# A Fourier mix and a squared-ReLU layer on one core: the order and size of the folding pieces on VectorE and ScalarE

## The chip, the core and the metric

The kernel runs on one core of a Trainium2 chip. The core has five engines with a queue of instructions each: TensorE (PE in the profile, with PEld for its weight loads), VectorE (DVE), ScalarE (ACT), GpSimd (POOL) and SyncE (SP), which here issues the loads and stores. An engine works through its own queue in order and waits on semaphores for the others. TensorE writes its results to PSUM; VectorE and ScalarE read them there, GpSimd does not.

The metric is the device time of one execution in microseconds (us), the lower the better. Every time in this document is in us unless ns is written.

## What is computed

```python
def _attn_ref(x):                       # x: 8 x 3008 x 256, float32
    X = np.fft.fft(x, axis=1)
    X = np.fft.fft(X, axis=2)
    return X.real.astype(np.float32)

def _moe_ref(x, w_in, w_out):           # x: 24064 x 256; w_in 256 x 2048; w_out 2048 x 256
    h = x @ w_in
    r = np.maximum(h, 0.0)
    g = r * r
    return (g @ w_out).astype(np.float32)
```

The first result, as 24064 rows of 256, is the second function's x. The tables of cosines and sines are made on the host from the sizes alone.

## The kernel before

**Folding.** The 3008 rows of a batch are used four at a time: rows n, S-n, M-n and M+n (M is S/2) have the same cosines and sines up to sign, so their sums and differences are formed first. 753 such groups of four make seven tiles of up to 128 partitions (`class_tiles`; the first four are the classes of even and of odd-even n, the last three, from `ODD0`, the odd class). `fold(b, t)` returns the pieces of work for batch b and tile t, each with a cost in units that a planner uses:

- `f_s` and `f_d` (L345, L349): sums and differences of the rows, two at a time, 512 elements.
- `f_sc` and `f_dc` (L355, L356, L360): the same along the 256 columns, column d with column D-d; the columns 0 and 128, which have no partner, are copied (L355).
- `f_p` and `f_q` (L370, L375): the folded tile `w`, in two parts of the columns (`PART`: 129 and 127) and two parities kp.
- for tiles 5 and 6 of a later batch, which share a class that is split once more, `f_turn` (a shuffle on VectorE, a copy on ScalarE, L395), `f_even` (two VectorE operations, L407 and L408, then `sine`: four ScalarE multiplications, L403) and `f_odd` (two VectorE operations, L415, which read what `sine` wrote).

`f_d` also issues the load of the tile three places later.

**Transform.** `dft_ops(b)` lists the row transform in groups: matmuls (L440, L485) into `pd`, ScalarE copies (L448, L489) and VectorE sums and differences (L453 to L457, L497 to L501) into `Pt` and `Qt`, 1505 columns, and `Et` for the column 128, which is gathered from all later batches at once: `load_column` loads it (28 small DMAs), `fold_column` folds it tile by tile (L327, L330), `dft_ops(None)` transforms it.

**Layer.** The column transform is multiplied into w_in once (`G1`, `G2`, `gE`). Then each batch has six blocks of 251 columns of `Pt` and `Qt` (the last has 250) and each block eight steps j. The loop at the end goes through all 8 x 6 x 8 = 384 steps i. In a step, `front` does two halves: two matmuls into `ph` (L536, L537), then on VectorE `he` (L539) and the two parts of `g` (L541, L542), then a call of `between()`. After that come the stores that are due, then `back` for the step two before (`LAG` = 2): seven matmuls (L589) into the accumulators mA to mD, which exist once. Last comes `combine`: Relu and Square on ScalarE (L551, L552) and four GpSimd operations that make `s` (L559 to L562). After the eighth step of a block, `gather` copies mA and mB to SBUF on ScalarE (L605, L607) and combines them with mC and mD on VectorE (L610 to L612) and GpSimd (L614 to L622). Because of the lag this happens in the step with j = 1 of the next block; TensorE may begin mA of the new block, one step later, when L605 has read the old one. The two stores of a block follow in steps 3 and 4, with VectorE transposes (L649, L650) and DMAs on SP.

**The planner.** While batch b is in the loop, the pieces that prepare batch b+1 (`ahead`) are in the list `side`. `between()` takes `pace` from `spent` and, while `spent` is not above zero, takes pieces from the list and adds their cost. `pace` is the sum of the costs over the number of calls, less six. In the first batch it begins at step 8, at half pace for the first eight steps. Steps 0 to 7 still bring in the weights (`load_win`, `load_wout`), whose `convert` splits a float64 into float32 on VectorE and ScalarE (L227 to L240).

**The start.** Batch 0 has nothing to hide its preparation behind. The pieces are called in an order written out by hand: `for_p(t)` calls the pieces 0, 2 and 4 of tile t (s, sc, p), `for_q(t)` the pieces 1, 3 and 5, with groups of the transform between. Buffers: `fs`, `fd`, `sc`, `dc` two each (`fp`), `s` three (`sp`), PSUM's `h` and `d` two each.

Of the kernel before, what the change touches and what calls it, by code (L numbers as in the profile page):

```python
# [13 lines left out]
P = 128  # L14
# [67 lines left out]
def kernel(  # L82
# [120 lines left out]

    raws = 0

    def convert(dst, src):
# [4 lines left out]
        if src.dtype == F32:  # L211
            w = fp.tile([P, 2, CH], F32, name="fs", tag="fs")
# [10 lines left out]
        m = fp.tile([P, 2, CH], F32, name="fs", tag="fs")  # L223
# [22 lines left out]
    def load_win(j):  # L246
# [4 lines left out]
        def products():  # L251
# [11 lines left out]
            nc.scalar.copy(gE[:, j::NJ], ps[:, 0:2])  # L263
# [49 lines left out]
    xe, we = {}, {}  # L313
    e_dram = dp.tile([NE, NKT], F32, name="e_dram")

    def load_column(t):

        _, r0, step, rows = TILES[t]
        xe[t] = const.tile([P, 4, NE], F32, name=f"xe{t}")
        for i in range(4):  # L320
            nc.sync.dma_start(out=xe[t][0:rows, i], in_=x[1:B, r0:r0 + step * (rows - 1) + 1:step, i, H].rearrange("b r -> r b"))

    def fold_column(t):
        r = slice(0, TILES[t][3])
        v = xe[t]
        s = hp.tile([P, 2, NE], F32, name="es", tag="es", bufs=2)
        tt(out=s[r], in0=v[r, 0::2], in1=v[r, 1::2], op=ALU.add)  # L327
        we[t] = const.tile([P, 2, NE], F32, name=f"we{t}")
        for kp in range(2):
            tt(out=we[t][r, kp], in0=s[r, 0], in1=s[r, 1], op=ALU.subtract if kp else ALU.add)  # L330

    def fold(b, t):
# [10 lines left out]
        def f_s():  # L343
            v = xt[b, t]
            tt(out=new(fp, "fs", [P, 2, D])[r], in0=v[r, 0::2], in1=v[r, 1::2], op=ALU.add)  # L345

        def f_d():
            v = xt[b, t]
            tt(out=new(fp, "fd", [P, 2, D])[r], in0=v[r, 0::2], in1=v[r, 1::2], op=ALU.subtract)  # L349
            if b > 0 and b * NT + t + NX < B * NT:  # L350
                load_x(*divmod(b * NT + t + NX, NT))

        def f_sc():
            s, sc = st["fs"], new(fp, "sc", [P, 2, H + 1])
            nc.vector.tensor_copy(sc[r, :, 0:H + 1:H], s[r, :, 0:H + 1:H])  # L355
            tt(out=sc[r, :, 1:H], in0=s[r, :, 1:H], in1=s[r, :, D - 1:H:-1], op=ALU.add)  # L356

        def f_dc():
            d = st["fd"]
            tt(out=new(fp, "dc", [P, 2, H - 1])[r], in0=d[r, :, 1:H], in1=d[r, :, D - 1:H:-1], op=ALU.subtract)  # L360
# [6 lines left out]
        def f_p():  # L367
            sc, w = st["sc"], w_of(t)
            for kp in range(2):
                tt(out=w[r, kp, PART[0]], in0=sc[r, 0], in1=sc[r, 1], op=ALU.subtract if kp else ALU.add)  # L370

        def f_q():
            dc, w = st["dc"], w_of(t)
# [473 lines left out]
```

## Time and profile before

| what | us |
|---|---|
| median of 6 runs | 1968.94 |
| the runs | 1967.08 to 1969.64 |
| the profiled execution | 1967.04 |
| its span, first to last instruction | 1965.3 |

Busy time by stage, from the table of stretches (TensorE's granted clock is a share of full speed):

| stretch | PE | DVE | ACT | POOL | clock |
|---|---|---|---|---|---|
| 0 to 110: load, batch 0, first block | 83.06 | 92.40 | 53.08 | 0.71 | 0.94 |
| 110 to 245 (135 us): batch 1 prepared | 134.15 | 124.85 | 66.31 | 84.74 | 1.00 |
| 245 to 1655 (1410 us) | 1406.52 | 1067.01 | 668.90 | 899.23 | 1.00 |
| 1655 to the end (311 us) | 301.95 | 175.63 | 139.03 | 183.27 | 0.99 |

How to read it: a busy share says where an engine had an instruction under way. A matmul's record lasts longer than the distance to the next one (0.375 against 0.21), so short pauses of TensorE hide in the overlap, and the distance from start to start is the better measure. A line of the timeline gives the start, the time taken, engine, source line, operation, what is written from what, the count, and in brackets the idle time before it with what ended that. A line of the list of waits gives engine, tensor and line, what it waited for, the total, how often, and the longest.

### The profile page before, as it was taken

To read this page: it belongs to the slowest core of one execution; us is meant where nothing else is said; L and a number is where in the kernel's file an instruction comes from. 1 tells how busy PE (TensorE), PEld (TensorE's weight loads), DVE (VectorE), ACT (ScalarE), POOL (GpSimd) and SP (SyncE) were. 2 spreads that over 40 slices of the span, in tenths; PEclk is the share of its full clock that TensorE was granted. 3 is DMA by queue.
4 is the path that set the end of the run, shared out by engine and by line. 5 is a ranking of instruction groups with operands and counts; after the bars stand their busy time and mean duration, and the time that the engine had idled before them with its cause. 6 is when DMAs were issued, how large, how long until landed. Compare 5 with 4: busy or idle time off the path is not lost.

```text
span 1965.3 us, 27667 instructions
## 1 busy us (share of the span) xinstructions
PE 1925.7 (98%) x9160; PEld 1705.1 (87%) x9160; DVE 1459.9 (74%) x3606; ACT 927.3 (47%) x1075; POOL 1168.0 (59%) x1702
## 2 busy tenths in 40 slices
PE   5999999999999999999999999999999999999998
PEld 3788888888988889888898888888898888988887
DVE  7889967887678876887768886787867887655554
ACT  1754544454445544545444454444544454444443
POOL 0037645667466765676557665666756676556564
PEclk8999999999999999999999999999999999999999
DMA  7332101110011110111011100121001100000000
GB/s 197 108 45 52 27 13 44 45 27 25 29 34 33 32 25 27 41 35 33 11 35 37 45 19 11 37 52 27 20 16 51 33 11 22 27 11 11 22 11 22
DMA packets 145341, 68.89 MB, mean 35 GB/s; under 512 B 129003, under 2 KB 136110, under 8 KB 145197
## 3 DMA queue, kind: packets, MB, share of 16 engines
q1 hardware_dynamic: 144121, 66.60, 13.1%
q8 instruction: 72, 1.18, 0.3%
q14 instruction: 72, 0.59, 0.1%
q10 hardware_dynamic: 1076, 0.52, 0.1%
HBM read 42.39 MB, written 24.68 MB: 34 GB/s over the span
## 4 chain that ended last, share of the span: by engine, by line
PE 91%; DVE 5%; ACT 2%; DMA 1%; issue 1%; POOL 0%; SPq 0%; DVEq 0%; ACTq 0%; POOLq 0%
PE mA L589 16%; PE mC L589 16%; PE ph L537 16%; PE ph L536 16%; PE mB L589 16%; PE mD L589 8%; PE pd L440 2%; PE pd L485 2%; DVE he L539 1%; DVE g L542 1%; DVE g L541 1%; DMA cosT<-in_cos_s_dram 1%; ACT g L551 0%; ACT g L552 0%; DMA xt<-in_x_dram 0%
## 5 line engine op out<-in xcount | busy, mean ns | idle before, releaser
L551 ACT ACTIVATE g<-g 128x1004 f32<-128x1004 f32 (+1 forms) x384 | 399.3, 1040 | 797.9 <-DVE g L542 456.7
L559 POOL TENSOR_TENSOR s<-g 128x251 f32<-128x251 f32 (+1 forms) x376 | 241.2, 641 | 713.2 <-ACT g L552 675.9
L539 DVE SCALAR_TENSOR_TENSOR he<-Et,gE,ph 128x251 f32<-128x251 f32 (+1 forms) x768 | 361.2, 470 | 388.2 <-PE ph L537 387.3
L536 PE MATMUL ph<-Pt,G 128*128 128x251 f32 (+1 forms) x1536 | 451.4, 375 | 4.3 <-ACT G L256 3.4
L537 PE MATMUL ph<-Qt,G 127*128 127x251 f32 (+1 forms) x1536 | 451.3, 374 | 0.4 <-DVE Qt L453 0.4
L552 ACT ACTIVATE g<-g 128x1004 f32<-128x1004 f32 (+1 forms) x384 | 399.3, 1040 | 12.2
L589 PE MATMUL mA<-g,wout 128*128 128x251 f32 (+1 forms) x1504 | 380.4, 374 | 3.5 <-ACT sA L605 3.5
L589 PE MATMUL mC<-s,wsum 128*128 128x251 f32 (+1 forms) x1504 | 381.7, 375 | 0.0
L541 DVE TENSOR_TENSOR g<-he,ph 128x251 f32<-128x251 f32 (+1 forms) x768 | 320.4, 417 | 54.9 <-DVE he L539 1.0
L536 PEld LDWEIGHTS ph<-Pt,G 128*128 128x128 f32 x1536 | 288.2, 189 | 41.7 <-ACT G L256 4.0
L537 PEld LDWEIGHTS ph<-Qt,G 127*128 127x128 f32 x1536 | 291.1, 190 | 36.6 <-DVE Qt L453 0.8
L589 PEld LDWEIGHTS mA<-g,wout 128*128 128x128 f32 x1504 | 281.9, 189 | 40.0 <-ACT sA L605 5.8
L589 PEld LDWEIGHTS mC<-s,wsum 128*128 128x128 f32 x1504 | 285.7, 190 | 34.6
L542 DVE TENSOR_TENSOR g<-he,ph 128x251 f32<-128x251 f32 (+1 forms) x768 | 314.2, 409 | 0.0
L560 POOL TENSOR_TENSOR s<-s,g 128x251 f32<-128x251 f32 (+1 forms) x376 | 289.8, 771 | 29.5
L561 POOL TENSOR_TENSOR s<-g 128x251 f32<-128x251 f32 (+1 forms) x376 | 293.1, 780 | 0.0
L562 POOL TENSOR_TENSOR s<-g,s 128x251 f32<-128x251 f32 (+1 forms) x376 | 253.5, 674 | 0.0
L589 PE MATMUL mB<-g,wsum 128*128 128x251 f32 (+1 forms) x752 | 220.5, 374 | 0.0
L589 PE MATMUL mD<-s,wout 128*128 128x251 f32 (+1 forms) x752 | 220.3, 374 | 0.0
L589 PE MATMUL mB<-s,wout 128*128 128x251 f32 (+1 forms) x752 | 219.9, 374 | 0.0
L589 PEld LDWEIGHTS mB<-g,wsum 128*128 128x128 f32 x752 | 142.6, 190 | 17.4
L589 PEld LDWEIGHTS mD<-s,wout 128*128 128x128 f32 x752 | 141.9, 189 | 17.7
(117 smaller groups left out, 1354.4 us busy)
## 6 DMA issues: line engine op xcount, KB each, us to landing
out_dram<-os SPq DMA_DIRECT2D x376, 56.0 KB
xt<-in_x_dram SPq DMA_DIRECT2D x32, 384.0 KB
xt<-in_x_dram SPq DMA_DIRECT2D x42, 128.0 KB
Et<-e_dram SPq DMA_DIRECT2D x7, 752.5 KB
xt<-in_x_dram SPq DMA_DIRECT2D x9, 512.0 KB
out_dram<-os SPq DMA_DIRECT2D x288, 6.8 KB
raw<-in_moe_w_in_dram SPq DMA_DIRECT2D x16, 256.0 KB
raw<-in_moe_w_out_dram SPq DMA_DIRECT2D x16, 256.0 KB
```

What stands on the lines that cost most here:

```text
L536: nc.tensor.matmul(hP, G1[:, fs], pt[:, ks], start=True, stop=True)
L537: nc.tensor.matmul(hQ, G2[:, fs], qt[:, ks], start=True, stop=True)
L539: nc.vector.scalar_tensor_tensor(out=t, in0=et[:, ks], scalar=gE[:, fc:fc + 1], in1=hP, op0=ALU.mult, op1=ALU.add)
L541: tt(out=g[:, h, 0, 0:n], in0=t, in1=hQ, op=ALU.add)
L542: tt(out=g[:, h, 1, 0:n][:, ::-1], in0=t, in1=hQ, op=ALU.subtract)
L551: act(v, v, AF.Relu)
L552: act(v, v, AF.Square)
L559: gt(out=s1, in0=g21, in1=g22, op=ALU.add)
L560: gt(out=s2, in0=s1, in1=g11, op=ALU.subtract)
L561: gt(out=s3, in0=g11, in1=g21, op=ALU.subtract)
L562: gt(out=s4, in0=g12, in1=s2, op=ALU.subtract)
L589: nc.tensor.matmul(acc[nm][:, i, 0:n], w, v[:, 0:n], start=j == 0 and i == 0, stop=j == NJ - 1, skip_group_check=True)
```

## The change

- `fold`: column D of the sums is a column of zeros in two constant buffers (`sums`), so that one operation forms all 129 sums of `f_sc`; column 0 gets x + 0, column 128 gets twice its value. The differences are taken in another order (`0::3` less `1:3`), so that both parts of the columns have the same sign in the last step; for batches after the first, `f_sc` and `f_dc` write one tile and `f_w` forms all 256 columns of a parity in one operation. The costs are new.
- The factor two of column 128 is balanced: `gE` is halved where it is made, and the separately loaded columns are doubled (`nc.scalar.mul(xe, xe, 2.0)`). They lie in one tile `xe`, set to zero on GpSimd, and are folded in three VectorE operations for all seven tiles.
- `convert` takes its scratch from the pool of `s` rather than from `fs`.
- `sine` becomes a piece of its own, after `f_even` and before `f_odd`.
- `between()` does nothing in the steps with j = 1, and `pace` is worked out for the calls that are left.

```diff
+    sums = [const.tile([P, 2, D + 1], F32, name=f"fs{i}") for i in range(2)]
+    for v in sums:
+        nc.gpsimd.memset(v[:, :, D:], 0.0)
...
+    def scratch():
+        return sp.tile([P, 4 * CK], F32, name="m", tag="s")[:, 0:2 * CH].rearrange("p (c e) -> p c e", c=2)
...
-        m = fp.tile([P, 2, CH], F32, name="fs", tag="fs")
+        m = scratch()
...
-            nc.scalar.copy(gE[:, j::NJ], ps[:, 0:2])
+            nc.scalar.mul(gE[:, j::NJ], ps[:, 0:2], 0.5)
...
-    xe, we = {}, {}
+    xe = const.tile([P, 4, NT, NE], F32, name="xe")
+    we = const.tile([P, 2, NT, NE], F32, name="we")
+    nc.gpsimd.memset(xe, 0.0)
...
-    def fold_column(t):
-        r = slice(0, TILES[t][3])
-        v = xe[t]
-        s = hp.tile([P, 2, NE], F32, name="es", tag="es", bufs=2)
-        tt(out=s[r], in0=v[r, 0::2], in1=v[r, 1::2], op=ALU.add)
-        we[t] = const.tile([P, 2, NE], F32, name=f"we{t}")
+    def fold_columns():
+        nc.scalar.mul(xe, xe, 2.0)
+        s = hp.tile([P, 2, NT, NE], F32, name="es", tag="es", bufs=1)
+        tt(out=s, in0=xe[:, 0::2], in1=xe[:, 1::2], op=ALU.add)
         for kp in range(2):
-            tt(out=we[t][r, kp], in0=s[r, 0], in1=s[r, 1], op=ALU.subtract if kp else ALU.add)
+            tt(out=we[:, kp], in0=s[:, 0], in1=s[:, 1], op=ALU.subtract if kp else ALU.add)
...
         def f_s():
+            nonlocal folds
+            st["fs"] = sums[folds % 2]
+            folds += 1
             v = xt[b, t]
-            tt(out=new(fp, "fs", [P, 2, D])[r], in0=v[r, 0::2], in1=v[r, 1::2], op=ALU.add)
+            tt(out=st["fs"][r, :, 0:D], in0=v[r, 0::2], in1=v[r, 1::2], op=ALU.add)
 
         def f_d():
             v = xt[b, t]
-            tt(out=new(fp, "fd", [P, 2, D])[r], in0=v[r, 0::2], in1=v[r, 1::2], op=ALU.subtract)
+            tt(out=new(fp, "fd", [P, 2, D])[r], in0=v[r, 0::3], in1=v[r, 1:3], op=ALU.subtract)
...
+        def halves():
+            if b == 0 or "sc" not in st:
+                st["sc"] = fp.tile([P, 2, D], F32, name="sc", tag="sc")
+            return st["sc"]
+
         def f_sc():
-            s, sc = st["fs"], new(fp, "sc", [P, 2, H + 1])
-            nc.vector.tensor_copy(sc[r, :, 0:H + 1:H], s[r, :, 0:H + 1:H])
-            tt(out=sc[r, :, 1:H], in0=s[r, :, 1:H], in1=s[r, :, D - 1:H:-1], op=ALU.add)
+            s = st["fs"]
+            tt(out=halves()[r, :, PART[0]], in0=s[r, :, 0:H + 1], in1=s[r, :, D:H - 1:-1], op=ALU.add)
 
         def f_dc():
             d = st["fd"]
-            tt(out=new(fp, "dc", [P, 2, H - 1])[r], in0=d[r, :, 1:H], in1=d[r, :, D - 1:H:-1], op=ALU.subtract)
+            tt(out=halves()[r, :, PART[1]], in0=d[r, :, 1:H], in1=d[r, :, D - 1:H:-1], op=ALU.subtract)
...
-        def f_p():
-            sc, w = st["sc"], w_of(t)
+        def f_w(part=slice(0, D)):
+            v, w = st["sc"], w_of(t)
             for kp in range(2):
-                tt(out=w[r, kp, PART[0]], in0=sc[r, 0], in1=sc[r, 1], op=ALU.subtract if kp else ALU.add)
-
-        def f_q():
-            dc, w = st["dc"], w_of(t)
-            for kp in range(2):
-                tt(out=w[r, kp, PART[1]], in0=dc[r, 0], in1=dc[r, 1], op=ALU.add if kp else ALU.subtract)
-
-        ops = [(0.9, f_s), (0.9, f_d), (1.2, f_sc), (0.6, f_dc), (0.9, f_p), (0.7, f_q)]
+                tt(out=w[r, kp, part], in0=v[r, 0, part], in1=v[r, 1, part], op=ALU.subtract if kp else ALU.add)
+
+        if b == 0:
+            return [f_s, f_d, f_sc, f_dc, lambda: f_w(PART[0]), lambda: f_w(PART[1])]
+        ops = [(0.9, f_s), (0.9, f_d), (0.7, f_sc), (0.6, f_dc), (1.1, f_w)]
...
             tt(out=v, in0=a, in1=w, op=ALU.add)
             tt(out=w, in0=a, in1=w, op=ALU.subtract)
+
+        def f_sine():
             sine(spare("f1", "f1"), st["w"], (0, 1))
             sine(spare("f2", "f0"), st["v"], (1, 0))
...
-        return ops + [(0.8, f_turn), (1.2, f_even), (1.4, f_odd)]
+        return ops + [(0.8, f_turn), (1.3, f_even), (0.2, f_sine), (1.4, f_odd)]
...
-        return (folds + [start] + [(0.6, lambda t=t: fold_column(t)) for t in range(NT)] + dft_ops(None) + tables
+        return (folds + [start] + [(1.5, fold_columns)] + dft_ops(None) + tables
...
-        if i < NJ:
+        if i < NJ or i % NJ == LAG - 1:
             return
...
-                spent, pace = 0.0, sum(t for t, _ in side) / (2 * per - 6 - (0 if i else 3 * NJ))
+                calls = 2 * (NJ - 1) * len(BLOCKS) - 6
+                spent, pace = 0.0, sum(t for t, _ in side) / (calls - (0 if i else 3 * (NJ - 1)))
```

## The prediction

> **What bounds the kernel now.** I read the page first (engine shares, the 40 slices), then TensorE's own waits after 110 us, then the timelines of PE, ACT and DVE around each wait, last the start. The page:
>
> ```profile
> span 1965.3 us, 27667 instructions
> ...
> PE 1925.7 (98%) x9160; PEld 1705.1 (87%) x9160; DVE 1459.9 (74%) x3606; ACT 927.3 (47%) x1075; POOL 1168.0 (59%) x1702
> ...
> PE   5999999999999999999999999999999999999998
> ...
> PE 91%; DVE 5%; ACT 2%; DMA 1%; issue 1%; POOL 0%; SPq 0%; DVEq 0%; ACTq 0%; POOLq 0%
> ```
>
> TensorE is the bound from the second slice to the last but one; VectorE, whose folds the diff rewrites, has a quarter of the span free. So VectorE time saved is worth nothing by itself; only TensorE's stalls and the start can give. TensorE's waits from 110 us to the end:
>
> ```profile
> PE mA L589 <- ACT sA L605: 3.5, 6, 0.8
> PE ph L536 <- DVE g L542: 0.8, 2, 0.7
> PE po L638 <- DVE c L616: 0.5, 1, 0.5
> ```
>
> Nine waits in 1855 us; the third is the tail, which the diff leaves alone. The six of the first line lie about 235 us apart (478, 712, 947, 1181, 1416, 1651), one per batch that is prepared. One of them, PE then ACT:
>
> ```profile
> 712.17 0.59 PE L537 MATMUL ph<-Qt,G 127*128 127x251 f32 x2
> 713.29 1.11 PE L589 MATMUL mA<-g,wout 128*128 128x251 f32 x4 [0.54 <-ACT sA L605]
> 714.25 0.38 PE L589 MATMUL mB<-g,wsum 128*128 128x251 f32 x1
> ...
> 712.09 0.69 ACT L403 ACTIVATE f<-w,turn 60x129 f32<-60x129 f32 x2 [1.97 <-DVE w L408]
> 712.69 0.56 ACT L605 COPY sA<-mA 128x502 f32<-128x502 f32 x1
> ```
>
> TensorE may not start the new block's mA before ScalarE has copied the old one (L605). ScalarE had stood still for 1.97 us in front of the second pair of multiplications of `sine`, since these wait for VectorE's L408, and L605 is queued behind them. A pair of matmuls normally starts every 0.425 us (four 0.85). Here mA starts 713.29-712.17=1.12 after the pair before, 0.69 late, and mB 0.96 after mA, 0.11 late: the stall costs 0.80 us, more than the idle 0.54. Five are like this; the sixth (1650.50 to 1651.90, then 0.96) costs 0.97+0.11=1.08. Sum 5.08.
>
> The second line of waits, PE:
>
> ```profile
> 239.76 0.59 PE L537 MATMUL ph<-Qt,G 127*128 127x251 f32 x2
> 241.05 0.69 PE L536 MATMUL ph<-Pt,G 128*128 128x251 f32 x2 [0.70 <-DVE g L542]
> ...
> 211.30 0.59 PE L537 MATMUL ph<-Qt,G 127*128 127x251 f32 x2
> 212.04 0.69 PE L536 MATMUL ph<-Pt,G 128*128 128x251 f32 x2 [0.15 <-DVE g L542]
> ```
>
> Counted alike, 1.29-0.43+0.10=0.96 and 0.74-0.43+0.10=0.41. In both VectorE was behind: from 236.96 to 239.75 it does the tiny `fold_column` operations, and at 212 the `even` pair and two transposes.
>
> **The change, part by part.** *(a) ScalarE's sine later, gather steps free.* The step counter can be replayed from the code. Before: 54.2 units over 90 calls is 0.602 a call; ahead of the last `f_even` stand 40.6 units, so it is popped at call 68, step 33 of 48, and 33 mod 8 = 1 is the step with the gather: exactly the six stalls. After: 47.8 units over 78 calls, 0.613 a call, 14 calls per block; ahead of the last `f_sine` stand 35.2, call 58, the second call of step 32, one step before the gather; `f_even` goes at step 31. So L408 is long done, and in step 32 ScalarE has 1.4 us of sine (two rows of 0.69) and 2.1 us of Relu and Square in 4.67 us, nothing else ahead of L605. **-5.08.**
>
> What is late next? The other tile: `f_sine` (27.3 units ahead, call 45) and `f_odd` (27.5, call 45) are popped in one call, the first of step 26, just after a gather step. VectorE's L415 waits there for ScalarE, with half 1's he and g queued behind it, and TensorE's next ph for those. From the clean gather step that starts at 631.41: sA starts 2.75 later, sB ends 4.2 later; Relu and Square (1.04 each) then end at 6.3, the two sine pairs at 7.0 and 7.65. VectorE has half 0's g at 7.05 and ends two L415 (0.72 mean) by 8.5, half 1's three (1.2) by 9.7; TensorE needs them at 10.2. Margin 0.5, so 0; range 0 to 0.4 for each of seven batches.
>
> *(b) Fewer fold operations in the main loop.* Per tile, L355 goes (0.27 mean), four L370/L375 (0.53 and 0.58) become two of 256 elements. No such row exists; L407 and L408, same shape, take 0.47 and 0.81 in the mean. So a tile costs 5.26 now and 3.72 to 4.41 after. Hidden behind TensorE; it matters only while batch 1 is prepared, where VectorE is 93% busy (110 to 210 us). A block of eight steps has 37.4 us; 16 halves of 1.16, the gather's three (1.2) and four transposes (1.7) leave 15.9. Before, 16 calls of 0.976 units at 1.01 us: 15.8, hence the 0.41 stall. After, 14 calls of 0.970 at 0.89 to 1.05: 12.1 to 14.3. Both L536 stalls should go, **-0.41** and, since `fold_columns` is 3 DVE operations (nearest row 128x94 0.25) for 21, **-0.96**. Its ScalarE multiplication (128x196; between 0.19 of 128x1 and 0.50 of 128x377) comes a step after the gather, before VectorE gets there; its DMAs were issued 90 us earlier, in the same places on SP's queue. But steps 26 to 28 are the heaviest: each 2.3 for the halves, then sc, dc and w (1.9 to 2.9); turn, even and two transposes (2.5 to 3.2); odd and two transposes (2.3). Added up with a step of 4.67, the carry into step 29 is 0.1 to 1.4, and there half 1's g, with the next f_s (0.85) in front, comes 1.2 before TensorE needs it or 0.2 after. I take **+0.2** (0 to 0.8, about half of the two stalls).
>
> *(c) The start.* Up to 20 us everything waits for the cosT DMA, so the first five L355 gave nothing. Two more are on the path (DVE, DVE, PE):
>
> ```profile
> 25.29 0.17 DVE L355 COPY sc<-fs 128x4 f32<-128x4 f32 x1
> ...
> 28.06 0.17 DVE L355 COPY sc<-fs 120x4 f32<-120x4 f32 x1
> ...
> 29.08 5.13 PE L440 MATMUL pd<-cosT,w 120*128 120x377 f32 x14 [1.15 <-DVE w L370]
> ```
>
> Each takes 0.21 from its start to the next one's, so L440 starts 0.42 earlier and VectorE, which is never idle for 0.3 from 33.5 to 52.3, carries that on. The granted clock was 0.50 from 20 to 30 us and 0.77 from 30 to 35, that is, it rose at about 32.3. If the rise follows the matmuls, 0.42 is gained; if it stays, the six cold matmuls after 29.1 (0.63 each, warm 0.32) gain about half. I take **-0.25**, midway, range 0 to -0.5. [...] From 53 to 106 us the loop of 8.5 us a step (Relu, Square, G, fd, then win, he, g) keeps all its members; gE as a multiplication rather than a copy is 0.19 (128x1 row) against 0.175, **+0.1** over six. The conversions' scratch tile only moves to the pool of s, which GpSimd first uses at step 8, when the conversions are over. Three memsets on an idle GpSimd before 9 us: 0.
>
> **Sum**: -5.08-0.41-0.96+0.2-0.25+0.1 = -6.4 against this execution's 1967.04 (span 1965.3 and 1.7 around it): 1960.6. The median of the runs shown, 1968.94, is 1.9 above the profiled one, and the start's clock can explain such a spread; I carry the difference over: **1962.5 us**.
>
> [...]
>
> **Rivals.**
> 1. VectorE's stalls in batch 1's preparation stay or come back between steps 26 and 35: for it: the same units in seven steps of eight; against it: 12.1 to 14.3 of 15.9 us above. Only (a) and (c) are left, 5.2: 1963.7; with one new 1 us stall 1964.7. 15%.
> 2. sine and odd in one call: ScalarE's half a microsecond of margin is not there. Each 0.3 to 0.5 late, seven times, gives back 2.1 to 3.5: 1964.6 to 1966.0, within 0.2%. For: in the step of the example Relu started 0.6 after sB's end (636.18); against: it followed g of half 1 (ended 636.09), which an f_s of 1.2 us had held up, and step 25 has no piece now. 12%.
> 3. Slower: the same place, decided where ScalarE ends sine over 1.4 us later than worked out (0.5 of margin and 6.4/7=0.9 of gain). With 2.5 late, 2.0 times 7 is 14 lost, 7.6 net: 1976.5. For: the list of waits puts waits of up to 3.3 us before L551 down to GpSimd; against: these are ends of idle time in which g was not there either. 6%.
> [...]
>
> The forecast has 62%: all eight stalls gone, less up to 0.8, 1961.3 to 1964.0. For eight in ten I reach over rivals 1, 4 and most of 2: **1960.6 to 1966.0**. A measurement of this kernel tells about 0.2%, 3.9 us, from no change; that is 1965.0. Faster: the forecast, rival 4, four fifths of 1 and a fifth of 2, less a little for run-to-run spread (the six runs span 2.6): 0.80. Same 0.13, slower 0.07.
>
> **What would show it.** Waits of mA on sA after 110 us: none left (six before). Waits of ph on g: at most one, under 0.4. ScalarE's L403 rows done a step before L605, without a wait for the second of `even`. VectorE busy under 1420 us, TensorE's busy time as before. Matmuls at 28.7 rather than 29.1. Wrong if ph waits for g appear once a batch about 40 us before the old stalls (rivals 2 and 3), or if L605 is still late.

## The result, and the profile after

The changed kernel takes 1963.71 us in the median (1961.27 to 1966.65) against 1968.57 for the kernel before, measured beside it: 0.9976 of the time, 95% interval 0.9970 to 0.9983. The profiled execution took 1962.59. Lines of the changed kernel are shifted: `back` is L604, the copy sA is L620, ph is L551 and L552, he is L554, g is L556 and L557, `f_w` is L386, `sine` is L416.

The page after; the lines are the span and the busy time of each engine, with its share and its number of instructions:

```profile
span 1960.8 us, 27513 instructions
...
PE 1924.9 (98%) x9160; PEld 1705.0 (87%) x9160; DVE 1399.4 (71%) x3434; ACT 925.0 (47%) x1076; POOL 1170.2 (60%) x1705
```

TensorE's busy time is what it was (1925.7 before) with the same 9160 matmuls. VectorE lost 60 us of busy time and 172 instructions, far more than the 4.9 us that the kernel gained; most of it was hidden and stayed so. TensorE's waits from 110 us to the end (engine, tensor and line, what it waited for, total, times, longest):

```profile
PE ph L551 <- DVE g L557: 0.8, 1, 0.8
PE po L653 <- DVE c L631: 0.5, 1, 0.5
```

The six waits of mA on sA are gone. One wait of ph on g is left, of 0.8, as much as the two of before together; the other line is the tail. Here is ScalarE near 709 us, in the timeline of the changed kernel, where the stall was at 713 before:

```profile
703.33 1.26 ACT L416 ACTIVATE f<-w,turn 60x129 f32<-60x129 f32 x4
705.06 1.04 ACT L566 ACTIVATE g<-g 128x1004 f32<-128x1004 f32 x1 [0.47 <-POOL s L575]
706.13 1.04 ACT L567 ACTIVATE g<-g 128x1004 f32<-128x1004 f32 x1
708.84 0.58 ACT L620 COPY sA<-mA 128x502 f32<-128x502 f32 x1 [1.66 <-PE mA L604]
```

All four multiplications of `sine` run in one go (x4, no bracket, so no wait), a step before the copy, and sA is now ready to go 1.66 us before TensorE has finished what it copies. Before, sA was the one that was late.

Rivals 2 and 3 of the prediction are about step 26, where `sine` and `odd` of the other tile come in one call. VectorE there in the second batch, and TensorE at the start of step 27:

```profile
442.17 1.45 DVE L430 SCALAR_TENSOR_TENSOR w<-w,turn,f 128x256 f32<-128x256 f32 x2 [0.34 <-ACT f L416]
...
444.37 0.41 DVE L557 TENSOR_TENSOR g<-he,ph 128x251 f32<-128x251 f32 x1
```

```profile
444.98 0.59 PE L551 MATMUL ph<-Pt,G 128*128 128x251 f32 x2
```

The g of half 1 ends at 444.78, 0.20 before the ph that needs it; over the six batches from the second on it is 0.12 to 0.20. TensorE does not wait, but it is close.

Where the time went, by stage, from the starts of the ph matmuls in TensorE's timeline. "Batches" are the six distances from one batch's first ph to the next one's, from the second batch on:

| kernel | first ph | steps 0 to 8 | steps 8 to 48 | batches | from the last batch's first ph to the end |
|---|---|---|---|---|---|
| before | 51.34 | 60.41 | 205.63 | 234.58 to 234.59 five times, 234.86 | 240.11 |
| after | 51.84 | 60.42 | 205.68 | 233.75 to 233.92 | 240.13 |

The batches give 1407.76-1402.73 = 5.03 us. Steps 8 to 48, where batch 1 is prepared and where the prediction expected 1.17, gave nothing. So the gain in time is the gain of the batches, and the rest of the question is what made it, what took back the second term, and what became of the start.

### The profile page after: what moved, and what is told of

The parts are those of the page before. It is cut to its first block, busy times and chain, and to the rows that moved or that the text cites. A ratio compares the mean times of both kernels' runs of the same rounds, so it can differ in the third digit from the quotient of the medians.

```text
span 1960.8 us, 27513 instructions
## 1 busy us (share of the span) xinstructions
PE 1924.9 (98%) x9160; PEld 1705.0 (87%) x9160; DVE 1399.4 (71%) x3434; ACT 925.0 (47%) x1076; POOL 1170.2 (60%) x1705
## 4 chain that ended last, share of the span: by engine, by line
PE 93%; DVE 4%; ACT 1%; DMA 1%; issue 0%; SPq 0%; DVEq 0%; ACTq 0%
PE ph L552 16%; PE ph L551 16%; PE mC L604 16%; PE mA L604 16%; PE mB L604 16%; PE mD L604 8%; PE pd L455 2%; PE pd L500 2%; DVE he L554 1%; DVE g L557 0%; DVE g L556 0%; DMA cosT<-in_cos_s_dram 0%; ACT g L566 0%; ACT g L567 0%; DMA xt<-in_x_dram 0%
## 5 line engine op out<-in xcount | busy, mean ns | idle before, releaser
L574 POOL TENSOR_TENSOR s<-g 128x251 f32<-128x251 f32 (+1 forms) x376 | 246.1, 655 | 715.8 <-ACT g L567 658.2
L554 DVE SCALAR_TENSOR_TENSOR he<-Et,gE,ph 128x251 f32<-128x251 f32 (+1 forms) x768 | 361.8, 471 | 421.5 <-PE ph L552 420.4
L551 PE MATMUL ph<-Pt,G 128*128 128x251 f32 (+1 forms) x1536 | 451.8, 375 | 4.2 <-ACT G L263 3.4
L552 PE MATMUL ph<-Qt,G 127*128 127x251 f32 (+1 forms) x1536 | 451.4, 374 | 0.4 <-DVE Qt L468 0.4
L604 PE MATMUL mC<-s,wsum 128*128 128x251 f32 (+1 forms) x1504 | 381.4, 374 | 0.0
L604 PE MATMUL mA<-g,wout 128*128 128x251 f32 (+1 forms) x1504 | 379.8, 374 | 0.0
L556 DVE TENSOR_TENSOR g<-he,ph 128x251 f32<-128x251 f32 (+1 forms) x768 | 320.5, 417 | 54.4 <-POOL s L574 0.5
L551 PEld LDWEIGHTS ph<-Pt,G 128*128 128x128 f32 x1536 | 287.3, 189 | 42.2 <-ACT G L263 4.0
L552 PEld LDWEIGHTS ph<-Qt,G 127*128 127x128 f32 x1536 | 291.2, 190 | 36.6 <-DVE Qt L468 0.8
L604 PEld LDWEIGHTS mC<-s,wsum 128*128 128x128 f32 x1504 | 285.5, 190 | 34.6
L557 DVE TENSOR_TENSOR g<-he,ph 128x251 f32<-128x251 f32 (+1 forms) x768 | 314.2, 409 | 0.0
L604 PEld LDWEIGHTS mA<-g,wout 128*128 128x128 f32 x1504 | 282.8, 189 | 34.7 <-issue 0.6
L575 POOL TENSOR_TENSOR s<-s,g 128x251 f32<-128x251 f32 (+1 forms) x376 | 283.3, 754 | 29.4
L576 POOL TENSOR_TENSOR s<-g 128x251 f32<-128x251 f32 (+1 forms) x376 | 295.2, 785 | 0.0
L604 PE MATMUL mB<-g,wsum 128*128 128x251 f32 (+1 forms) x752 | 220.5, 374 | 0.0
L604 PE MATMUL mD<-s,wout 128*128 128x251 f32 (+1 forms) x752 | 220.3, 374 | 0.0
L604 PE MATMUL mB<-s,wout 128*128 128x251 f32 (+1 forms) x752 | 219.9, 374 | 0.0
L604 PEld LDWEIGHTS mB<-g,wsum 128*128 128x128 f32 x752 | 142.6, 190 | 17.4
L604 PEld LDWEIGHTS mD<-s,wout 128*128 128x128 f32 x752 | 141.9, 189 | 17.7
```

The costliest lines, as they stand in the source:

```text
L551: nc.tensor.matmul(hP, G1[:, fs], pt[:, ks], start=True, stop=True)
L552: nc.tensor.matmul(hQ, G2[:, fs], qt[:, ks], start=True, stop=True)
L554: nc.vector.scalar_tensor_tensor(out=t, in0=et[:, ks], scalar=gE[:, fc:fc + 1], in1=hP, op0=ALU.mult, op1=ALU.add)
L556: tt(out=g[:, h, 0, 0:n], in0=t, in1=hQ, op=ALU.add)
L557: tt(out=g[:, h, 1, 0:n][:, ::-1], in0=t, in1=hQ, op=ALU.subtract)
L574: gt(out=s1, in0=g21, in1=g22, op=ALU.add)
```

## The experiments

In the table, "sA waits" are TensorE's listed waits of mA on sA, and "ph waits" those of ph on g, in one profiled execution each, from 110 us on. Ratios are to the kernel before, measured beside it; its medians there were 1968.35 (e1 to e4), 1968.33 (e5 to e7), 1968.44 (e8) and 1967.26 (e9). A ratio is not the quotient of the medians, which for e7 would be 0.9978. The kernel with the columns by tile has a single run and no ratio. The stretches repeat well where the program is the same: e7 differs from the changed kernel only in the start, and its steps 8 to 48 take 205.66 against 205.68.

| kernel | time, us | ratio | sA waits | ph waits | steps 8 to 48 | batches |
|---|---|---|---|---|---|---|
| before | 1968.57 | 1 | 6, 3.5 us | 2, 0.8 us | 205.63 | 234.58, one 234.86 |
| after | 1963.71 | 0.9976 (0.9970 to 0.9983) | none | 1, 0.8 us | 205.68 | 233.75 to 233.92 |
| e1_sine_piece | 1965.10 | 0.9986 (0.9977 to 0.9995) | none | 3, 1.4 us | 206.41 | 233.78 to 233.79 |
| e2_gather_free | 1964.77 | 0.9984 (0.9975 to 0.9992) | none | 3, 1.5 us | 207.35 | 233.78 |
| e3_folds_only | 1964.21 | 0.9981 (0.9972 to 0.9990) | none | 3, 1.1 us | 206.08 | 233.74 to 233.77 |
| e4_w_in_two | 1962.65 | 0.9974 (0.9965 to 0.9983) | none | none | 204.43 | 233.75, one 234.03 |
| e5_sine_at_gather | 1965.02 | 0.9983 (0.9974 to 0.9992) | none | 4, 1.8 us | 207.06 | 233.74 to 233.77 |
| e6_columns_by_tile | 1964.45 (one run) | none | none | 3, 1.3 us | 206.24 | 234.01 twice, 233.72 |
| e7_more_copies | 1964.06 | 0.9966 (0.9952 to 0.9979) | none | 1, 0.8 us | 205.66 | 233.71 to 233.75 |
| e8_even_at_gather | 1965.35 | 0.9985 (0.9975 to 0.9994) | none | 2, 1.0 us | 206.07 | 233.80 to 233.98 |
| e9_even_second_call | 1970.04 | 1.0011 (1.0001 to 1.0020) | 6, 1.9 us | 3, 1.1 us | 206.05 | 234.57 to 234.62 |

### Each part alone

The kernel before, with `sine` as a piece of its own:

```diff
             tt(out=w, in0=a, in1=w, op=ALU.subtract)
+        def f_sine():
             sine(spare("f1", "f1"), st["w"], (0, 1))
...
-        return ops + [(0.8, f_turn), (1.2, f_even), (1.4, f_odd)]
+        return ops + [(0.8, f_turn), (1.0, f_even), (0.2, f_sine), (1.4, f_odd)]
```

> The kernel before with one edit: the sine multiplications are a piece of their own behind f_even (costs 1.0 and 0.2 instead of 1.2, so every other piece is popped where it was). Theory A (the six stalls are sine waiting for L408 with L605 queued behind it): f_even of the last tile stays in the gather step, sine goes one call later, behind L605; no wait of mA on sA is left after 110 us, the two waits of ph on g (0.41 and 0.96) stay, total -5.1 us, ratio 0.9974. Theory B (the gather step is overfull on VectorE and ScalarE, whatever waits for what): the six waits stay or shrink by less than half, -0 to -2.5 us. A also says that the distance between two batches' starts falls from 234.57 to about 233.77.

The kernel before, with no pieces in the gather steps:

```diff
-        if i < NJ:
+        if i < NJ or i % NJ == LAG - 1:
             return
...
+                calls = 2 * (NJ - 1) * len(BLOCKS) - 6
+                spent, pace = 0.0, sum(t for t, _ in side) / (calls - (0 if i else 3 * (NJ - 1)))
```

> The kernel before with one edit: no pieces in the steps with j = 1, and the pace for the calls left; sine stays in f_even, the folding is the old one. Theory A: f_even with sine of the last tile moves from the gather step to the first call of step 34, behind L605: six waits of mA on sA gone, -5.1 us. In batch 1's preparation the same old VectorE work is put into seven eighths of the calls (pace 1.13 units a call for 0.98), where by my sum 15.8 of 15.9 us were used before: theory A expects more waits of ph on g there, 0.5 to 3 us more than the 1.4 of before; so 1964 to 1966.5 in all. A theory in which free gather steps are worth something of their own expects fewer such waits.

The changed kernel with both of these undone, so that only the folds and their costs are new:

```diff
-        return ops + [(0.8, f_turn), (1.3, f_even), (0.2, f_sine), (1.4, f_odd)]
+        return ops + [(0.8, f_turn), (1.5, f_even), (1.4, f_odd)]
...
-        if i < NJ or i % NJ == LAG - 1:
+        if i < NJ:
```

> The changed kernel with the sine put back into f_even (cost 1.5) and the pieces allowed in the gather steps again: the folding part alone. The costs alone move the last f_even from step 33 to step 31 (33.9 units ahead at 0.531 a call: call 64). Theory A: the six waits of mA on sA are gone here too, though no ScalarE edit is left, since they hung on which call the piece falls in; -5.1 us of 1968.6, with the new wait of ph on g at step 18 (about 1.0 in the changed kernel's profile) still there: 1963.5. Theory C (the ScalarE edits are what removed them): the six waits are back, 1968.

Each of the three takes all six waits away, and brings the batches from 234.58 to 233.74-233.79. The third has neither of the two edits that were aimed at ScalarE: with its costs `f_even` of tile 6 is popped at call 64, in step 31, instead of call 68. So the 5 us are not a sum of parts. They are one gain, which any of three edits brings, and the other two then bring nothing there. The time of the first fell short of its expectation (0.9986 for 0.9974). Batch 1 took back 0.78 of the 5.1, which the expectation had not foreseen; what the rest is, stays open. The second lies where it was expected.

What differs is batch 1. Freeing the gather steps packs the same old folds into seven steps of eight, and steps 8 to 48 grow from 205.63 to 207.35. The three waits of ph on g that this variant keeps:

```profile
PE ph L536 <- DVE g L542: 1.5, 3, 0.8
PE po L638 <- DVE c L616: 0.5, 1, 0.5
```

That is 1.7 us back for the freed steps with the old folds. With the light folds it is the other way round: with pieces in the gather steps (e5_sine_at_gather, next) steps 8 to 48 take 207.06, without them 205.68.

### Was it the wait of sine, or sine itself?

The changed kernel with pieces allowed again in the gather steps, so that `sine` and `f_odd` stand in them:

```diff
-        if i < NJ or i % NJ == LAG - 1:
+        if i < NJ:
...
+                spent, pace = 0.0, sum(t for t, _ in side) / (2 * per - 6 - (0 if i else 3 * NJ))
```

> The changed kernel with the pieces of the folding allowed again in the steps where a block's results are gathered; sine stays a piece of its own. Replayed by its costs, the sine and odd pieces of tile 6 then both fall on the first call of the gather step 33 and those of tile 5 on the second call of the gather step 25, long after VectorE's even. This separates two readings of the six waits of mA on sA. Theory A: it was the wait of sine for VectorE's even that held the copies sA up; ScalarE stands idle for 1.3 to 1.7 us ahead of sA in a clean gather step (1.66 at 708.84 of the changed kernel) and sine's two rows take 1.3, so sine fits in and no wait of mA on sA comes back, or seven small ones of at most 0.3 (0 to 2 us in all; 1963 to 1965.5). Theory B: the 1.3 us of sine themselves in the gather step hold sA up, whatever they wait for: six or seven waits of 0.5 to 1 come back (4 to 7 us, 1967 to 1970). VectorE's two odd operations in the gather step (1.4 us) may give ph a wait for g of 0.1 to 0.5 by either theory.

ScalarE's timeline of that kernel, in a gather step:

```profile
711.19 1.26 ACT L416 ACTIVATE f<-w,turn 60x129 f32<-60x129 f32 x4
712.94 0.58 ACT L620 COPY sA<-mA 128x502 f32<-128x502 f32 x1 [0.49 <-PE mA L604]
```

The four multiplications stand directly ahead of sA, and sA still waits for TensorE (0.49 us), not for them. No wait of mA on sA came back and the batches are 233.74 to 233.77. In step 25 the pieces of tile 5 fall on the second call, the harmful one, and there too sA is done at 676.93, 2.25 before TensorE starts mA. So the 1.26 us of `sine` fit into the gather step; the wait inside it did the harm. The part of the change that keeps pieces out of gather steps was not needed for this gain; in batch 1 it is worth 1.38 (207.06 against 205.68).

### Putting the stall back

If the place of `f_even` alone decides, a change of cost that moves it back must bring the stall back, with the light folds. First, on the variant with the folds alone:

```diff
-        return ops + [(0.8, f_turn), (1.5, f_even), (1.4, f_odd)]
+        return ops + [(6.0 if i else 0.8, f_turn), (1.5, f_even), (1.4, f_odd)]
```

> The variant with the folds alone (sine inside f_even, pieces allowed in the gather steps), with one number changed: the cost of f_turn for tile 6 is 6.0 and not 0.8, which does no work but moves f_even of tile 6, replayed by its costs, from call 64 (step 31) to the first call of step 33, the step with the gather, where it stood in the kernel before; f_odd of tile 6 goes to step 34. The folds stay the light ones. Theory A (the six waits come from where f_even falls: L605's copy is queued behind the second pair of sine, which waits for VectorE's second operation of even): the waits of mA on sA are back, six of 0.5 to 0.8 (3 to 5 us listed), the distances between the starts of the batches go from 233.75 to 234.4 to 234.7, and the time is 4 to 6 us above that of the variant with the folds alone: 1968 to 1970. Rival (the heavy old folds are needed as well, since they made VectorE late with even): no wait of mA on sA or six below 0.3, distances below 234.0, the time within 1.5 us of that variant's 1964.2. The denser pieces of batch 1 may add up to 1 us of ph waiting for g by either.

No stall came, and by the words of the expectation that speaks for the rival. But the expectation had misplaced the old stall: it put `f_even` on the first call of the step, and in the kernel before it was the second. ScalarE's timeline of this variant:

```profile
709.58 0.69 ACT L416 ACTIVATE f<-w,turn 60x129 f32<-60x129 f32 x2 [2.09 <-DVE w L421]
710.18 0.56 ACT L618 COPY sA<-mA 128x502 f32<-128x502 f32 x1
```

The wait of `sine` is there, with its 2.09 us, and sA is queued behind it without a gap. But sA ends at 710.74, and TensorE's next mA is due at 712.17: 1.43 us of room. A wait that is just as long makes TensorE wait for nothing when it begins one call earlier (the batches are 233.80 to 233.98). A second variant moves it to the second call, with the costs of the pieces that come after the folds:

```diff
-            return folds + dft_ops(b) + [(0.0, lambda: load_e(b))]
+            return folds + [(0.75 * c, f) for c, f in dft_ops(b)] + [(0.0, lambda: load_e(b))]
```

> The variant with the folds alone (sine inside f_even, pieces allowed in the gather steps), and from the third batch on the costs of the transform's pieces, which come after the folds, times 0.75. No work changes; replayed by its costs, f_turn of tile 6 then falls on the first call of the gather step 33 and f_even on the second, as in the kernel before. (The variant with the cost 6.0 had f_even on the first call: sA then ended 1.4 before TensorE wanted mA, and in the kernel before VectorE's f_even began 2.05 later, measured from the step's matmuls.) Theory A (the call on which f_even falls decides, whatever the folds weigh): six waits of mA on sA, 0.5 to 0.8 each, distances between the starts of the batches from the second on 234.4 to 234.7 for 233.75, and 4 to 5.5 us more than the 1964.2 of the variant with the folds alone: 1968 to 1970. Rival (the old, heavy folds are needed too): no such waits, or below 0.3, and 1963 to 1965.5.

The kernel does the same work as the variant with the folds alone, and takes 1970.04 instead of 1964.21 (1.0011 and 0.9981 of the kernel before beside each), no less than the kernel before. TensorE's waits:

```profile
PE mA L602 <- ACT sA L618: 1.9, 6, 0.3
PE ph L549 <- DVE g L555: 1.1, 3, 0.4
```

The batches are back at 234.57 to 234.62, that is 0.83 more each, six times, 5.0 us. The place of the pieces is enough, with the light folds too. The sizes were not as expected: the waits listed are 0.3 and not 0.5 to 0.8. They lie eight steps earlier, where tile 5 has come to stand in the same way on a gather step (25). TensorE, VectorE and ScalarE there:

```profile
678.37 0.59 PE L550 MATMUL ph<-Qt,G 127*128 127x251 f32 x2
679.26 1.11 PE L602 MATMUL mA<-g,wout 128*128 128x251 f32 x4 [0.30 <-ACT sA L618]
```

```profile
676.54 0.65 DVE L420 TENSOR_TENSOR w<-f,w 128x256 f32<-128x256 f32 x1
677.22 0.74 DVE L421 TENSOR_TENSOR w<-f,w 128x256 f32<-128x256 f32 x1
```

```profile
678.05 0.69 ACT L416 ACTIVATE f<-w,turn 128x129 f32<-128x129 f32 x2 [1.83 <-DVE w L421]
678.66 0.55 ACT L618 COPY sA<-mA 128x502 f32<-128x502 f32 x1
```

In order of time: VectorE ends the second of `even` at 677.96, ScalarE's second pair starts 0.09 later, sA follows it, and mA starts 679.26-678.37 = 0.89 after the pair of matmuls before it instead of 0.43. With the 0.10 that the next matmuls lose, that is 0.56. In step 33 the stall is only 0.26 (0.16 by the starts of TensorE's matmuls, and 0.10), where the two `even` operations there take 0.41 and 0.42 and not 0.63 and 0.73 as before. So step 33 alone gave back a third of the old stall, and step 25, which the expectation had not reckoned with, the rest. The call decides whether there is a stall; how long VectorE takes over `even` just then fits its size: the pair is 0.53 shorter in step 33 than before, and the stall 0.54 smaller.

### What took back the second term

The new stall of ph on g stands at 157.36, in step 17. TensorE of the changed kernel, then VectorE:

```profile
156.01 0.59 PE L552 MATMUL ph<-Qt,G 127*128 127x251 f32 x2
157.36 0.69 PE L551 MATMUL ph<-Pt,G 128*128 128x251 f32 x2 [0.76 <-DVE g L557]
```

```profile
151.57 0.71 DVE L282 TENSOR_TENSOR wsum<-wout 128x128 f32<-128x128 f32 x1
152.31 0.29 DVE L283 TENSOR_TENSOR wout<-wout 128x128 f32<-128x128 f32 x1
...
153.18 0.47 DVE L554 SCALAR_TENSOR_TENSOR he<-Et,gE,ph 128x251 f32<-128x251 f32 x1
...
154.44 1.70 DVE L386 TENSOR_TENSOR w<-sc 94x256 f32<-94x256 f32 x2
156.07 0.46 DVE L554 SCALAR_TENSOR_TENSOR he<-Et,gE,ph 128x251 f32<-128x251 f32 x1
...
156.90 0.41 DVE L557 TENSOR_TENSOR g<-he,ph 128x251 f32<-128x251 f32 x1
```

Two things make half 1 of step 16 late, and TensorE waits for it in step 17. L282 to L285 (`sum_wout`, four operations in each of steps 8 to 15) run from 151.57 on and hold up half 0 until 153.18. Then `f_w`, which is one piece now, puts 1.63 us ahead of half 1, whose g ends at 157.31. TensorE's ph starts right behind it, 1.35 after the pair before. An `f_w` about as long (1.59 and 1.60) stands at 168.69 and 203.43, where `sum_wout` is over: TensorE lost 0.13 behind the first and nothing behind the second. To see what the size of the piece does, the changed kernel with `f_w` cut into its two operations:

```diff
-        def f_w(part=slice(0, D)):
+        def f_w(part=slice(0, D), kps=range(2)):
...
-        ops = [(0.9, f_s), (0.9, f_d), (0.7, f_sc), (0.6, f_dc), (1.1, f_w)]
+        ops = [(0.9, f_s), (0.9, f_d), (0.7, f_sc), (0.6, f_dc)] + [(0.55, lambda kp=kp: f_w(kps=(kp,))) for kp in range(2)]
```

> The changed kernel with f_w as two pieces of 0.55, one for each parity, instead of one of 1.1. Theory D (the 0.92 us late ph at 157 us comes from two contended 256-element operations, 1.63 us, as one lump between the two halves of step 16, in the stretch in which sum_wout puts 1.5 us more on VectorE in each step): only one of the two lies between the halves, half 1's g comes 0.8 earlier, the wait falls from 0.92 to 0.1 to 0.3, the sum of what TensorE loses between 110 and 245 us from 1.5 to 0.5 to 0.9; total -0.6 to -1.0 against the changed kernel. Theory E (VectorE is simply overfull there): the loss stays at 1.2 to 1.6, somewhere else. The rest as in the changed kernel: no wait of mA on sA.

TensorE's waits of that kernel from 110 us, the whole list:

```profile
PE po L653 <- DVE c L631: 0.5, 1, 0.5
PE ph L551 <- ACT G L263: 0.5, 1, 0.5
```

No wait of ph on g is left. (The second line is the end of the start: before and after it stands ahead of 110 us, and this execution started later.) Steps 8 to 48 take 204.43: 1.25 less than after and 1.20 less than before, close to the -1.17 that the prediction gave the change itself. The same operations, the same `sum_wout`; the unit in which they are queued is half as large. VectorE's timeline of this kernel at that place:

```profile
158.73 0.84 DVE L386 TENSOR_TENSOR w<-sc 94x256 f32<-94x256 f32 x1
159.50 0.46 DVE L554 SCALAR_TENSOR_TENSOR he<-Et,gE,ph 128x251 f32<-128x251 f32 x1
...
160.66 0.41 DVE L386 TENSOR_TENSOR w<-sc 94x256 f32<-94x256 f32 x1
```

One operation before half 1 and one after it, so half 1 starts 0.77 behind `f_w` and not 1.63. The second operation is also shorter here, 0.41 for 0.93, and the fourteen of batch 1 together take 8.2 for 10.1 us; how much of the 1.25 comes from this was not tried. This kernel has the lowest median, 1962.65, at a ratio of 0.9974; the times do not separate it from the changed kernel (0.9976), the traces do. Its profiled execution took 1966.04, since it had the latest start of all (below).

The other part of the term was the column 128, folded in three operations for 21. The same variant, with the columns folded tile by tile again:

```diff
-    def fold_columns():
-        nc.scalar.mul(xe, xe, 2.0)
+    def fold_column(t):
+        if t == 0:
+            nc.scalar.mul(xe, xe, 2.0)
...
-        return (folds + [start] + [(1.5, fold_columns)] + dft_ops(None) + tables
+        return (folds + [start] + [(0.6, lambda t=t: fold_column(t)) for t in range(NT)] + dft_ops(None) + tables
```

> The variant with f_w in two pieces, but the column 128 of all batches folded tile by tile again: 21 tiny VectorE operations in seven pieces for three in one. It prices the one part of step (b) that the prediction credited with 0.96. Theory A: the tiny operations (start to start about 0.2, so 4.2 us for 0.8) put VectorE behind again about steps 33 to 36, and ph waits for g by 0.3 to 1.0 there; the rest is as in the variant with f_w in two pieces. Rival: with the other folds lighter VectorE has room for them, and the list of TensorE's waits from 110 us is the same as without them (two lines: po for c and one ph of 0.5 for G).

Theory A had the cost and missed the place; the rival had neither. TensorE waits three times, for 1.3 us in all, and steps 8 to 48 grow by 1.81 over the kernel without the tiles, but the stalls are at 143.56, 158.64 and 182.58, in the folds, and none is at the columns (from 232 on):

```profile
PE ph L552 <- DVE g L558: 1.3, 3, 0.8
PE po L654 <- DVE c L632: 0.5, 1, 0.5
```

Seven pieces at 0.6 add 2.7 units of cost to the list. By the code the pace of the whole batch rises with them, and so the folds, 10 to 18 steps earlier, are popped closer together. That this is the cause is read from the code and the places of the stalls; no run held the pace as it was. In this planner, then, a piece can cost time where it pushes the others, and not where it stands itself.

### The start

The changed kernel with more VectorE work in the start, which changes nothing in the output:

```diff
             tt(out=halves()[r, :, PART[0]], in0=s[r, :, 0:H + 1], in1=s[r, :, D:H - 1:-1], op=ALU.add)
+            if b == 0 and t >= 5:
+                for k in range(8):
+                    nc.vector.tensor_copy(more[r, :, 2 * k:2 * k + 2], s[r, :, k:k + 2])
```

> The changed kernel with work added in its start and the result untouched: eight more VectorE copies of two by two elements into a tile that nobody reads, in each of the pieces for_p(5) and for_p(6), where the removed copies L355 stood that the prediction counted at -0.25. 16 copies at 0.17 to 0.21 from start to start are 2.7 to 3.4 us. Theory A (VectorE is on the path there, as the prediction had it): the time grows by half to all of that, 1.4 to 3.4 us, ratio to the changed kernel 1.0007 to 1.0017; the two removed copies were then worth a sixteenth to an eighth of it, 0.2 to 0.4. Rival: transfers and the granted clock set the start; the time stays within 0.7 us of the changed kernel's, and the distances between the starts of the batches stay as they are by either.

The copies were cheaper than expected: eight took 0.66 us (x8 in one row), and each group put off the operation behind it by only 0.44, both by 0.88. How far they reach is read from VectorE's fs of tile 5 to the first matmul of the group that needs `for_p(5)` and `for_p(6)`. VectorE and TensorE after, then in this kernel:

```profile
22.38 0.68 DVE L356 TENSOR_TENSOR fs<-xt 128x512 f32<-128x512 f32 x1
```

```profile
26.48 4.06 PE L455 MATMUL pd<-cosT,w 120*128 120x377 f32 x16 [0.56 <-DVE w L386]
```

```profile
23.69 0.69 DVE L357 TENSOR_TENSOR fs<-xt 128x512 f32<-128x512 f32 x1
```

```profile
28.67 4.06 PE L459 MATMUL pd<-cosT,w 120*128 120x377 f32 x16 [1.61 <-DVE w L390]
```

The distance is 4.10 after and 4.98 with the copies: all 0.88 arrives at TensorE. Before it is 29.08-24.57 = 4.51. So VectorE is on the path up to there, and the two removed copies gave 0.41, as worked out. They do not arrive in the time: the median with the copies (1964.06) is within the noise of the changed kernel's. The first place where they are lost is a load. VectorE's next conversion of weights, before, after and with the copies:

```profile
37.07 0.43 DVE L227 TENSOR_SCALAR fd<-raw 128x512 uint32<-128x512 uint32 x1
```

```profile
36.15 0.43 DVE L234 TENSOR_SCALAR fd<-raw 128x512 uint32<-128x512 uint32 x1 [1.96 <-DMA raw<-in_moe_w_in_dram]
```

```profile
36.34 0.43 DVE L234 TENSOR_SCALAR fd<-raw 128x512 uint32<-128x512 uint32 x1
```

The changed kernel waits there 1.96 us for the weights, the other two do not. With the copies the group begins 2.19 later than after (28.67 and 26.48), and this conversion only 0.19 later (36.34 and 36.15). Of the eight profiles of the changed kernel and of e1 to e7, six have this wait, with 0.68 to 1.96 us. After it the granted clock differs. From the group's first matmul to the first ph it is 22.26 before, 25.36 after, 26.09 with the copies and 27.94 in the variant with `f_w` in two. The stretch table of that last variant (stretch, length, PE, PEld, DVE, ACT, POOL, granted clock, DMA share, GB/s):

```profile
40.00:45.00 5.00, 4.13 (x8) 2.40 (x9) 3.25 (x10) 0.18 (x2) 0.00 (x0) 0.50 0.05 19
...
50.00:55.00 5.00, 5.00 (x9) 2.65 (x9) 4.16 (x9) 2.02 (x3) 0.00 (x0) 0.50 0.52 158
```

The granted clock fell to half again, after 38.8 us and after 49.0 us; in the changed kernel after 39.3. In the profiled execution of the kernel before it stayed at 1.00 from 35 us on, up to the tail (1960.8). The last matmuls of that part, the kernel before and that variant:

```profile
47.45 4.04 PE L440 MATMUL pd<-sinT,w 128*127 128x377 f32 x12 [2.28 <-ACT raw L234]
```

```profile
49.71 7.07 PE L455 MATMUL pd<-sinT,w 128*127 128x377 f32 x12 [2.19 <-ACT fd L237]
```

The same twelve matmuls take 4.04 or 7.07. Over the profiled executions the first ph lies at 51.3 to 56.6, and the kernels with the old start are no later than the others (51.34, 53.37 and 52.65). Gains of 0.2 to 0.4 can't be seen in that.

## Why the prediction was right, and where not

The time, the side and the range were right: 1962.5 predicted, 1963.71 measured. The sum of the terms was -6.4, the measured difference of the medians is -4.86, and the 1.5 between them is mostly one term, in (b). That the time missed by only 1.2 is partly chance: the kernel before was measured 0.37 lower this time (1968.57 for 1968.94).

- **(a), -5.08: right.** The batches gave 5.03. The mechanism is the one given: sA queued behind `sine`, which waits for VectorE's second `even`. It is shown from three sides: taking it away by any of three edits removes the waits, `sine` without its wait is harmless in the same step, and moving nothing but the calls on which pieces fall, so that `f_even` of both tiles stands on the second call of a gather step, brings 5.0 us back. What the prediction did not see is that the cheaper costs of the folds alone would have done it. The step "one step before the gather" for `sine` came out as worked out (703.33, then sA at 708.84).
- **(b), -0.41 -0.96 +0.2: the step that failed.** Both old stalls went, but new ones took their place: steps 13, 14, 17 and 20 of the changed kernel are 0.18, 0.19, 1.02 and 0.13 longer than the usual 4.67, 1.52 us for the +0.2. The prediction looked for VectorE's lateness in steps 26 to 29. It summed a block as a budget (12.1 to 14.3 of 15.9 us), which holds in the sum, but the limit is what stands between two halves of one step: `f_w` as one piece of two 256-element operations is 1.63 us there, at a place where `sum_wout`, which the budget left out, had just made VectorE late. Cutting the piece in two gave the expected gain. What `sum_wout` adds, here and in the small losses of steps 13 and 14, is read from the timeline; no run takes it out.
- **(b), the price of the new operation: right in its bounds.** The 256-element L386 takes 0.72 in the mean while batch 1 is prepared (10.1 us for 14), between the 0.47 and 0.81 taken from L407 and L408, but single ones reach 0.94.
- **(c), -0.25: right up to the group, wrong behind it; +0.1: not seen.** The group starts 0.41 earlier relative to VectorE's chain, for 0.42 worked out. But the prediction let VectorE carry this on to 52.3, since before it was never idle for 0.3 there. After, it stood still for 1.96 us at 36.15, waiting for weights, and for 1.34 at 43.27, waiting for TensorE, whose matmuls ran at half the clock from 39.3 to 42.8. Whether any of the 0.41 reaches the end can't be read off, since the first ph moves by up to 5 us between executions. The -0.25 was an estimate between a clock whose rise follows the matmuls and one whose rise stays, and no run shows its size. What two profiles show: the granted clock rose to full at 32.3 before and at 25.7 after, which is 12.1 and 7.7 behind the transform's first matmul (20.13 and 18.02), so not at a fixed distance from it; after, it fell again at 39.3. Steps 0 to 8, where the +0.1 lies, took 60.42 for 60.41.
- **Rival 1** (VectorE's stalls come back while batch 1 is prepared, 1963.7 to 1964.7) described this part better than the forecast did, and its lower figure is the measured median; it was given 15%. Its place (steps 26 to 35) was wrong too.
- **Rivals 2 and 3** (`sine` and `odd` in one call make ph wait in step 26, seven times) did not occur: no wait of ph on g is listed after batch 1. But the margin was 0.12 to 0.20, less than half of the 0.5 worked out: the working had VectorE begin `odd` when half 0's g was done, and it waited 0.34 more for `sine`.
- **Rival 4** (the start's clock rises earlier, 1 to 2 us more; 5%): the gain was the author's estimate. In the profiled execution the clock rose 6.6 us earlier (25.7 for 32.3) and fell back at 39.3, and the first ph came 0.5 later than before (51.84 for 51.34).

## What to carry to other kernels

When a stall comes back once per period, find which instruction on the releasing engine stands in front of the late one, and what that one waits for. A wait of about the same length (1.97 and 2.09) cost 0.8 us on the second call of a step, and no wait of TensorE on the first. When several edits each move an instruction off such a place, their gains do not add, and a later change of any cost in the same planner can bring the stall back: the same work took 1964.21 and 1970.04. And for fillers between deadlines the size of the largest piece counts, and not the sum per block alone: two operations queued as one piece cost 1.25 us more than as two.

## What the runs showed of the hardware that was not expected

- The granted clock did not stay up once it had risen: in the start it fell to half for 3.4 or 6.8 us at a time, at 37 to 41 us and later (in e1_sine_piece at 28.7 too). In the profiles of before and after its changes lie 3.41 us or a multiple of that apart. TensorE did not have to stand still all the while: in the 3.41 us ahead of the fall it had matmuls under way for none of it at 39.3 after, for about 1.5 at 28.7 in e1_sine_piece, and for about 2.0 at 38.8 in e4_w_in_two, where the last of them ended about 0.9 ahead of the fall. What makes the clock fall, no run shows. In the eight profiles of after and of e1 to e7 the first ph came later than before, by 0.5 to 5.3 us.
- VectorE's operation of 256 elements a partition with both inputs in SBUF took 0.41 or 0.42 where GpSimd was idle for nearly all of it, and 0.49 to 0.94 where GpSimd was at work for most of it (L386 of the changed kernel from 110 to 245: three of the first kind, eleven of the second). No run takes GpSimd's work away there.
- Tiny VectorE copies follow one another much faster than a single row shows: eight copies of 128x4 took 0.66 in all, about 0.07 from one to the next, where a lone one takes 0.17.
- After a wait TensorE loses about 0.10 us more: the pair of ph that had waited at 157.36 is 0.53 from the next pair (157.89), where 0.42 is usual, and 0.10 or 0.11 stands behind each stall priced above.
